# First key weights in three transfers, first x block in four parts, and a newly found order of work

## The chip, the cores and the metric

The kernel runs on one core of one Trainium2 chip. The metric is the device time of one execution in microseconds (us). It is given as the median of several runs. A profile is one execution recorded by the hardware profiler. It has a span, from the first to the last instruction, and an own time a little longer than the span.

A core has five engines with an instruction queue each: TensorE (PE in the views, with PEld for its weight loads), VectorE (DVE), ScalarE (ACT), GpSimd (POOL) and SyncE (SP). ACT and SP also issue DMA transfers here.

## The reference

The input x has 2048 tokens of 512 features in bf16. The output mixes two branches of the same x by a gate for each token:

```python
g = _sigmoid((x * gate_w).sum(-1, keepdims=True))
a = _A_ref(x, A_wq, A_wk, A_wv, A_wo, A_beta)
b = _B_ref(x, B_w_gate, B_w_up, B_w_down)
return g * a + (1 - g) * b
```

Branch A is attention with 32 heads of 16 features in four segments of 512 tokens. In each segment there is causal softmax attention inside the segment, and a read of a memory that the earlier segments have filled:

```python
logits = jnp.einsum('bhqd,bhkd->bhqk', qs, ks) * scale + mask
a_dot = jnp.einsum('bhqk,bhkd->bhqd', _softmax(logits, axis=-1), vs)
a_mem = (phi(qs) @ M) / (phi(qs) @ z + 1e-06)     # M, z: sums over earlier segments
o = g * a_mem + (1.0 - g) * a_dot                 # g = sigmoid(beta), for each head
M, z = M + phi(ks)^T @ vs, z + sum(phi(ks))
```

Here phi(t) is t + 1 where t is positive and exp(t) elsewhere. The heads are joined and multiplied by wo. Branch B is a gated feed-forward layer of width 1792: (gelu(x @ w_gate) * (x @ w_up)) @ w_down.

## The kernel before

The kernel is a list of some thousand small tasks. Each task is one step on one engine and is a handful of instructions. The functions below create the tasks. A long string, ORDER, gives the sequence in which they are written to the queues: each engine's queue holds its own tasks in the sequence of that string, and waits on semaphores are worked out from what each instruction reads and writes. A word such as `K0_1a:1` opens a PSUM bank (bank 1 of four, psD0 to psD3), and `Kev0_1:d` says that this eviction runs on DVE (`:a` is ACT).

The names of tasks carry the segment first. For segment s there are:

- `ld_...`: loads. x of segment 0 comes in two ways. Its tokens 0 to 255 come as rows (`ld_x0_0` on SP, `ld_x0_1` on ACT) and are transposed by PE (`xtr0_`) and copied out (`xev0_`, line 795). Its tokens 256 to 511 come through two DMA transposes (`ld_x0_t2`, `ld_x0_t3`, line 361). The other segments come through DMA transposes (`ld_x1_2` and so on, line 345). Line 341 issues every plain load.
- `warm1` and `warm2` (line 383): matmuls on constants, for no result.
- `K`, `Q`, `V`, `G`, `U`: projections, four matmuls of 512 columns each (V: two halves of 256 columns). In segment 0 the key tile K0_t is cut into a (blocks 2 and 3 of the input features, first 256 tokens), b (blocks 0 and 1, first 256 tokens) and c (all blocks, last 256 tokens); these are the matmuls of line 477. `Kev`, `Qev`, `Vev`, `Gev` evict the PSUM bank (lines 442 and 443, 506 and 507).
- `kpada`, `kpadb` (line 488): keys with alternate heads masked out, on DVE, one pair for each key tile.
- `st` (line 602) fills the four-bank score tile psX, `exp` (line 609) takes the exponential of all 2048 columns on ACT, `msk` (line 615) applies the causal mask on POOL. psX exists once, so st, exp, st, exp run in turn, 18 times for each segment.
- `pv` (line 644): probabilities times values for two key tiles; `tp`, `pvp`, `ota`, `otm` normalise and turn the result on DVE.
- `phka`, `phkb`, `phkc` and `phq...`: phi of keys and queries (DVE, ACT, DVE). `ktr`, `otr`: DMA transposes on SP. `mz`, `mza`, `mzq`: the update of the memory. `nd`, `ndp`: the read of it. `vsh`: a shifted copy of the values by DMA.
- `gelu`, `gd` on ACT; `h` (line 720) on DVE; `out` (line 735) is the down projection, `wo` (line 749) the output projection, `wev`, `oev` combine both, `dma` stores 128 tokens.
- `gwz` (line 354, DVE) clears a small tile, into which `ld_gw` loads the gate weights; `gwtr` on PE turns them.

In the string before, SP's loads begin x0_0, wk1, x0_t2, x0_t3, wq0, wq1, gw, wv, wg0, then x of segment 1; ACT's begin x0_1, wk0, wg0b. `wk1` holds blocks 2 and 3 of the key weights, `wk0` blocks 0 and 1.

Of the kernel before, what the change touches and what calls it, by code (L numbers as in the profile page):

```python
# [248 lines left out]
def _build(es, nc, A_x, A_wq, A_wk, A_wv, A_wo, A_beta, B_w_gate, B_w_up, B_w_down, gate_w, out):  # L249
# [90 lines left out]
    def ld_w(name, eng, dst, src, writes, size, wait=(), **kw):  # L340
        load(name, eng, lambda e: e.dma_start(dst, src), writes, size=size, wait=[("ld", w) for w in wait], **kw)
# [40 lines left out]
    for name, n, cols in (("warm1", 45, 80), ("warm2", 7, 80)):  # L382
        one(name, PE, 3.0, [I(lambda e, cols=cols: e.matmul(BK[s0.i][:, 0:cols], ones, ones[:, 0:cols], start=True, stop=True),  # L383
                              [], [bk(s0)]) for _ in range(n)], bias=9000.0, opens=name == "warm1")
# [400 lines left out]
    for p in (1, 0):  # L785
        one(f"xtr0_{p}", PE, 4 * T_TR, [I(lambda e, q=q, kb=kb, p=p: e.transpose(
            XB[:, 1024 * p + (kb % 2) * 256 + q * 128:1024 * p + (kb % 2) * 256 + q * 128 + 128],
            pt[stage[0]][:, q, kb * 128:(kb + 1) * 128], ident[:, :]),
            [("xs", 0, 0), ("xs", 0, 1), ("pt", stage[0]), ("ident",)], [("X", p)]) for kb in (2 * p, 2 * p + 1) for q in (0, 1)])
# [3 lines left out]
        task(f"xev0_{p}", [  # L793
            (ACT, 0.477, [I(lambda e, dst=dst, xin=xin: e.activation(dst, xin, ACTF.Copy), [("X", p)], wr)]),
            (DVE, 0.335, [I(lambda e, dst=dst, xin=xin: e.tensor_copy(dst, xin), [("X", p)], wr)])], L_DVE)
# [149 lines left out]
```

## Time and profile before

| | |
|---|---|
| median of 3 runs | 263.94 us (263.4 to 263.95) |
| profiled execution, own time | 264.41 us |
| its span | 262.7 us |
| busy: PE, DVE, ACT, POOL | 254.5, 198.1, 203.2, 98.3 us |
| HBM read, written | 7.87 MB, 2.10 MB |
| exp on ACT (L609) | 72 of 1.88 us, 135.1 us in all |
| masks on POOL (L615) | 128 of 0.73 us, 91.7 us in all |

A row of a timeline gives the start, the time taken, the engine, the line of the kernel, the operation, what it writes and reads, and a count; in brackets stands the idle time before it and what ended that. An engine with a q behind its name is the queue that issues DMAs. A row of a group gives busy time and the mean duration in ns behind the bar, then idle time before such instructions. The duration of a matmul includes its way through the array, so that matmuls in a row overlap: their spacing is read from their starts. In a table of stretches each column after the length is busy time with a count in brackets, then the granted TensorE clock, the DMA share and GB/s. A landing time counts from the issue of a transfer to the end of its last piece.

### The profile page before, as it was taken

To read this page: it belongs to the slowest core of one execution; us is meant where nothing else is said; L and a number is where in the kernel's file an instruction comes from. 1 tells how busy PE (TensorE), PEld (TensorE's weight loads), DVE (VectorE), ACT (ScalarE), POOL (GpSimd) and SP (SyncE) were. 2 spreads that over 40 slices of the span, in tenths; PEclk is the share of its full clock that TensorE was granted. 3 is DMA by queue.
4 is the path that set the end of the run, shared out by engine and by line. 5 is a ranking of instruction groups with operands and counts; after the bars stand their busy time and mean duration, and the time that the engine had idled before them with its cause. 6 is when DMAs were issued, how large, how long until landed. Compare 5 with 4: busy or idle time off the path is not lost.

```text
span 262.7 us, 6672 instructions
## 1 busy us (share of the span) xinstructions
PE 254.5 (97%) x2815; PEld 122.6 (47%) x2849; DVE 198.1 (75%) x412; ACT 203.2 (77%) x171; POOL 98.3 (37%) x163
## 2 busy tenths in 40 slices
...
DMA packets 31990, 16.50 MB, mean 63 GB/s; under 512 B 21592, under 2 KB 31960, under 8 KB 31960
## 3 DMA queue, kind: packets, MB, share of 16 engines
...
q10 hardware_dynamic: 688, 0.85, 0.9%
q8 instruction: 22, 0.36, 0.6%
...
HBM read 7.87 MB, written 2.10 MB: 38 GB/s over the span
## 4 chain that ended last, share of the span: by engine, by line
PE 88%; DVE 6%; ACT 3%; issue 2%; DVEq 0%
PE psD L449 41%; PE psD L735 19%; PE psX L602 8%; PE psD L644 6%; PE psD L749 5%; PE psD L499 5%; PE psD L547 1%; ACT gb L698 1%; PE psD L383 1%; PE psD L477 1%; DVE kT L443 1%; DVE gb L443 1%; ACT pt L609 1%; PE psD L577 1%; DVE phk L461 1%
## 5 line engine op out<-in xcount | busy, mean ns | idle before, releaser
L609 ACT ACTIVATE pt<-psX 128x2048 bf16<-128x2048 f32 x72 | 135.1, 1877 | 28.3 <-PE psX L602 26.7
L615 POOL TENSOR_TENSOR pt<-pt,ctri 128x256 bf16<-128x256 bf16 x128 | 91.7, 727 | 129.4 <-ACT pt L609 124.9
L449 PE MATMUL psD<-xT,wu 128*128 128x512 bf16 x214 | 52.7, 380 | 1.3 <-issue 1.1
L449 PE MATMUL psD<-xT,wg 128*128 128x512 bf16 x216 | 52.3, 379 | 0.8 <-issue 0.3
L735 PE MATMUL psD<-wd,gb 128*128 128x512 bf16 x217 | 51.8, 379 | 0.8 <-issue 0.5
L720 DVE TENSOR_TENSOR gb<-psD,gb 128x512 bf16<-128x512 f32 x56 | 37.2, 681 | 10.8 <-PE psD L449 10.8
L449 PEld LDWEIGHTS psD<-xT,wg 128*128 128x128 bf16 x224 | 20.7, 98 | 24.7 <-issue 1.3
L735 PEld LDWEIGHTS psD<-wd,gb 128*128 128x128 bf16 x224 | 20.7, 98 | 24.3 <-issue 2.1
L449 PEld LDWEIGHTS psD<-xT,wu 128*128 128x128 bf16 x224 | 20.2, 98 | 24.8 <-issue 2.6
L602 PE MATMUL psX<-qT,kD 32*128 32x192 bf16 (+7 forms) x512 | 28.5, 287 | 0.0
L530 DVE STREAM_TRANSPOSE tT<-psD 128x512 f32<-128x512 f32 x32 | 21.7, 701 | 5.5 <-PE psD L644 5.0
L443 DVE CAST gb<-psD 128x512 bf16<-128x512 f32 x20 | 13.6, 687 | 12.8 <-PE psD L449 12.8
L602 PEld LDWEIGHTS psX<-qT,kD 32*128 32x128 bf16 x512 | 8.2, 92 | 25.1 <-ACT pt L609 13.6
L499 PE MATMUL psD<-wv,xT 128*128 128x257 bf16 (+1 forms) x128 | 18.2, 273 | 0.0
L753 DVE SCALAR_TENSOR_TENSOR ost<-psD,gtok,wds 128x512 bf16<-128x512 f32 (+1 forms) x17 | 11.9, 710 | 7.9 <-PE psD L749 7.8
L668 DVE SCALAR_TENSOR_TENSOR ob<-tT,gq,rc 128x256 bf16<-128x256 f32 x32 | 16.7, 522 | 1.1
L703 ACT ACTIVATE gb<-psD 128x512 bf16<-128x512 f32 x28 | 15.0, 595 | 3.3 <-PE psD L449 3.3
L644 PE MATMUL psD<-pt,vsh 64*17 64x192 bf16 (+7 forms) x512 | 17.1, 283 | 0.0
L644 PE MATMUL psD<-pt,vnat 64*17 64x192 bf16 (+7 forms) x512 | 17.1, 283 | 0.0
L449 PE MATMUL psD<-xT,wq 128*128 128x512 bf16 x60 | 15.6, 379 | 0.4 <-issue 0.2
L749 PE MATMUL psD<-wo,oT 128*128 128x512 bf16 (+1 forms) x66 | 15.7, 367 | 0.2 <-issue 0.2
L499 PEld LDWEIGHTS psD<-wv,xT 128*128 128x128 bf16 x128 | 11.8, 97 | 6.6 <-issue 1.3
...
## 6 DMA issues: line engine op xcount, KB each, us to landing
out_dram<-ost SPq DMA_DIRECT2D x15, 128.0 KB, 1.9
...
wq<-in_A_wq_dram SPq DMA_DIRECT2D x2, 256.0 KB, 3.7
wv<-in_A_wv_dram SPq DMA_DIRECT2D x1, 512.0 KB, 3.8
wo<-in_A_wo_dram SPq DMA_DIRECT2D x1, 512.0 KB, 4.2
```

The source lines that it names most:

```text
L443: (DVE, 0.60, [I(lambda e: e.tensor_copy(dst, src()), [bk(sl), *reads], writes)]),
L449: one(name, PE, n * T_MM, [I(lambda e, i=i: e.matmul(BK[sl.i][:, :], lhs(i), rhs(i), start=(i == 0), stop=(i == n - 1)), reads(i), [bk(sl) ...
L499: one(f"V{s}_{m}{'ab'[hf]}", PE, 2 * T_MM, [I(lambda e, i=i, sl=sl, a=a, z=z, xs=xs: e.matmul(BK[sl.i][:, 0:z - a], xs(i), wv[:, i, a:z], ...
L530: one(f"tp{name}", DVE, 0.605, [I(lambda e, sl=sl, ti=ti: e.transpose(tT[ti][:, :], BK[sl.i][:, :]), [bk(sl)], [("tT", ti)])], bias=bias)
L602: ins.append(I(lambda e, t=t, kb=kb, ncol=ncol, c0=c0, g=g: e.matmul(XALL[:, g * 512 + c0:g * 512 + c0 + ncol], kD[(4 * s + t) % R_KD][32 ...
L609: one(f"exp{s}_{name}", ACT, 2048 * 0.000833 + 0.05, [I(lambda e: e.activation(pt[slot][:, :, :], xin, ACTF.Exp, scale=ATT_SCALE), [("X",) ...
L615: ins.append(I(lambda e, mv=mv: e.tensor_tensor(mv, mv, cm, ALU.mult), [("pt", slot), ("causal",)], [("pt", slot)]))
L644: ins.append(I(lambda e, kb=kb, slot=slot, c0=c0, n=n, g=g, r0=r0, sl=banks[j], va=va: e.matmul(BK[sl.i][32 * g:32 * g + 17, 64 * kb:512], ...
L668: I(lambda e, ti=ti, ri=ri, t=t, j=j, dst=dst: e.scalar_tensor_tensor(out=dst, in0=t_rows(ti), scalar=gq[:, 2 * t + j:2 * t + j + 1], in1= ...
L720: one(f"h{s}_{ft}", DVE, 0.605, [I(lambda e, sl=sl, gi=gi, f=f: e.tensor_tensor(gb[gi][:, f, :], BK[sl.i][:, :], gb[gi][:, f, :], ALU.mult ...
L735: mm.append(I(lambda e, fb=fb, gi=gi, f=f, q=q, sl=sl: e.matmul(BK[sl.i][:, :], gb[gi][:, f, q], wd[:, fb, :], start=(fb == 0), stop=(fb = ...
L749: one(f"wo{s}_{qt}{sfx}", PE, 4 * T_MM * w / 512, [I(lambda e, kb=kb, q=q, so=so, c=c, w=w: e.matmul(BK[so.i][:, 0:w], oT[:, kb, q], wo[:, ...
```

## The change

The key weights of blocks 2 and 3 are no longer one transfer on SP: block 2 stays there (`wk2`, 128 KB), block 3 goes to ACT (`wk3`, 128 KB), and blocks 0 and 1 (`wk0`, 256 KB) follow as ACT's third transfer. The two halves of the first x, `xtr0_1` and `xtr0_0` with one copy of 512 columns each, become four parts with one copy of 256 columns each, in four banks of psX; two of these copies run on ACT. The warm-up is one group of 52 matmuls of 66 columns in place of 45 and 7 of 80. ORDER is replaced as a whole. In the new string 46 evictions and copies run on ACT and 66 on DVE, where it was 35 and 75. Of the transfers, `gw` now follows `wg0`, `ktr0_0` comes early on SP, `ld_wo` comes after `vsh2_01`, and several `ktr`, `otr` and `vsh` trade places.

```diff
--- before.py
+++ after.py
@@ -355,8 +355,8 @@
     xin0 = A_x[0, 0:512, :].rearrange("(q p) d -> p q d", p=P)
     for eng, nm, q in ((SP, "0", slice(0, 1)), (ACT, "1", slice(1, 2))):
         ld_w(f"x0_{nm}", eng, pt[stage[0]][:, q, :], xin0[:, q, :], [("xs", 0, q.start)], 0.125)
-    for eng, h in ((SP, 1), (ACT, 0)):
-        ld_w(f"wk{h}", eng, wk[:, halves[h], :], wsrc(A_wk)[:, halves[h], :], [("wk", 2 * h), ("wk", 2 * h + 1)], 0.25)
+    for eng, nm, c in ((SP, "2", slice(2, 3)), (ACT, "3", slice(3, 4)), (ACT, "0", slice(0, 2))):
+        ld_w(f"wk{nm}", eng, wk[:, c, :], wsrc(A_wk)[:, c, :], [("wk", i) for i in range(c.start, c.stop)], 0.125)
     for q in (2, 3):
         load(f"x0_t{q}", SP, lambda e, q=q: e.dma_start_transpose(xT[0][:, :, 128 * q:128 * q + 128], A_x[0, 128 * q:128 * q + 128, :]),
              [("xT", 0, f"t{q}")], issue=1.31, lat=3.0)
@@ -379,9 +379,8 @@
 
     s0 = Slot()
     ones = nc.const_aps.tensor(1.0, [P, P], BF)
-    for name, n, cols in (("warm1", 45, 80), ("warm2", 7, 80)):
-        one(name, PE, 3.0, [I(lambda e, cols=cols: e.matmul(BK[s0.i][:, 0:cols], ones, ones[:, 0:cols], start=True, stop=True),
-                              [], [bk(s0)]) for _ in range(n)], bias=9000.0, opens=name == "warm1")
+    one("warm1", PE, 3.0, [I(lambda e: e.matmul(BK[s0.i][:, 0:66], ones, ones[:, 0:66], start=True, stop=True),
+                             [], [bk(s0)]) for _ in range(52)], bias=9000.0, opens=True)
     cn = [
         I(lambda e: e.memset(maskA[:], 0.0), writes=[("maskA",)]),
     ]
@@ -782,17 +781,15 @@
             I(lambda e: e.tensor_scalar(gfull[:], gfull[:], 1.0, None, ALU.add), [("gfull",)], [("gfull",)])], bias=-150.0)
 
     XB = XALL.bitcast(BF)
-    for p in (1, 0):
-        one(f"xtr0_{p}", PE, 4 * T_TR, [I(lambda e, q=q, kb=kb, p=p: e.transpose(
-            XB[:, 1024 * p + (kb % 2) * 256 + q * 128:1024 * p + (kb % 2) * 256 + q * 128 + 128],
+    for kb in (2, 3, 0, 1):
+        one(f"xtr0_{kb}", PE, 2 * T_TR, [I(lambda e, q=q, kb=kb: e.transpose(
+            XB[:, 1024 * kb + q * 128:1024 * kb + q * 128 + 128],
             pt[stage[0]][:, q, kb * 128:(kb + 1) * 128], ident[:, :]),
-            [("xs", 0, 0), ("xs", 0, 1), ("pt", stage[0]), ("ident",)], [("X", p)]) for kb in (2 * p, 2 * p + 1) for q in (0, 1)])
-        dst = xT[0][:, 2 * p:2 * p + 2, 0:256]
-        xin = XB[:, 1024 * p:1024 * p + 512].rearrange("p (k c) -> p k c", c=256)
-        wr = [("xT", 0, kb, "h0") for kb in (2 * p, 2 * p + 1)]
-        task(f"xev0_{p}", [
-            (ACT, 0.477, [I(lambda e, dst=dst, xin=xin: e.activation(dst, xin, ACTF.Copy), [("X", p)], wr)]),
-            (DVE, 0.335, [I(lambda e, dst=dst, xin=xin: e.tensor_copy(dst, xin), [("X", p)], wr)])], L_DVE)
+            [("xs", 0, 0), ("xs", 0, 1), ("pt", stage[0]), ("ident",)], [("X", kb)]) for q in (0, 1)])
+        dst, xin, wr = xT[0][:, kb, 0:256], XB[:, 1024 * kb:1024 * kb + 256], [("xT", 0, kb, "h0")]
+        task(f"xev0_{kb}", [
+            (ACT, 0.38, [I(lambda e, dst=dst, xin=xin: e.activation(dst, xin, ACTF.Copy), [("X", kb)], wr)]),
+            (DVE, 0.25, [I(lambda e, dst=dst, xin=xin: e.tensor_copy(dst, xin), [("X", kb)], wr)])], L_DVE)
 
     head_gates()
     for s in range(NSEG):
 ORDER = """
-ld_x0_0 ld_wk1 ld_x0_1 warm1:0 ident xtr0_1 xev0_1:d xtr0_0 warm2 xev0_0:d vones0 masks ld_wk0 causal1 gwz ld_x0_t2 ld_x0_t3 ld_wq0 ld_wq1 ld_gw
-causal0 consts K0_1a:1 K0_3a:2 K0_3b K0_2a:3 K0_0a:0 K0_2b K0_0b K0_1b K0_0c K0_2c K0_3c K0_1c Kev0_0:d Kev0_2:d kpadb0_0 kpadb0_2 causal kpada0_0
-Kev0_3:a Q0_0:0 ld_wg0b Qev0_0:a Q0_1:3 st0_0A gwtr:2 Kev0_1:d gwev Q0_3:0 ld_wv ld_wg0 Qev0_1:d V0_1b:1 V0_3a:2 V0_3b:3 exp0_0A Qev0_3:d Vev0_3a:a
-Vev0_1b:a st0_0B Vev0_3b:d kpada0_2 kpada0_1 V0_0b:0 V0_1a:2 V0_2a:1 Vev0_0b:d G0_6:3 Gev0_6:d Vev0_1a:d Vev0_2a:d exp0_0B st0_0C exp0_0C Q0_2:0
-G0_2:3 V0_2b:2 ld_x1_2 ld_x1_1 ld_x1_3 ld_x1_0 ld_beta st0_0D Vev0_2b:a exp0_0D Gev0_2:d kpadb0_1 Qev0_2:d phka0_0 V1_2b:1 V0_0a:3 G1_6:2 V1_0b:0
-Vev1_2b:d phka0_2 st0_0E Vev0_0a:d Vev1_0b:d G0_1:1 Gev1_6:a exp0_0E Gev0_1:d Q1_2:3 V1_3b:2 V1_3a:0 kpada0_3 Qev1_2:d Vev1_3a:d phkb0_2 phkc0_2
-Vev1_3b:d st0_1A gz0 exp0_1A gr0 Q1_0:1 V1_0a:3 G1_5:0 Vev1_0a:d Gev1_5:d st0_1B Q1_1:2 K1_0:3 exp0_1B phkb0_0 ld_wu1 ld_x2_0 G0_5:0 Qev1_0:d kpadb0_3
-vsh0_21 st0_1C exp0_1C Qev1_1:d ld_x2_1 ld_x2_3 ktr0_3 ld_wg1 Gev0_5:d V1_2a:1 K1_3:2 K1_1:0 vsh0_01 Vev1_2a:a vsh0_20 ld_x2_2 ktr0_2 vsh0_00 ld_wd1
-st0_1D phkc0_0 betab Kev1_1:d kpada1_1 G0_4:1 G0_3:0 Gev0_4:d Kev1_0:d Gev0_3:d Kev1_3:a ld_wd0 ld_wu0 ktr0_1 ktr0_0 vsh1_20 ld_wo V1_1a:2 Vev1_1a:d
-exp0_1D bexp st0_2A exp0_2A msk0_0B msk0_0D msk0_0C kpada1_0 msk0_0E goa0 gob0 msk0_0A msk0_1A msk0_1C msk0_1D gqa gfull msk0_1B G0_0:1 Q1_3:3 G1_1:0
-Qev1_3:d phqa1_0 st0_2B Gev0_0:d gqb Gev1_1:a pv0_1:2301 exp0_2B tp0_d01 tp0_d00 pvp0_01 Q2_0:3 Qev2_0:d tp0_d11 st0_2C K1_2:2 Kev1_2:d pvp0_00
-tp0_d10 gelu0 G0_8:3 G0_13:1 gd0_13 G0_10:2 G0_11:0 G0_9:1 gd0_8 gd0_10 gd0_9 gd0_11 G0_12:3 G0_7:2 gd0_12 G1_2:1 U0_0:0 gd0_7 Gev1_2:d pvp0_11 h0_0
-U0_13:3 U0_10:2 h0_10 Q2_1:1 Qev2_1:d exp0_2C st0_2D mz0:0 U0_7:2 U0_9:1 pvp0_10 h0_13 exp0_2D phqb1_0 st0_2E exp0_2E phka1_0 h0_7 mza0 h0_9 ota0_0
-phqa1_2 kpadb1_0 G1_4:3 U0_1:2 h0_1 Gev1_4:a V1_1b:0 st0_3A G1_0:1 U0_5:3 Q2_2:2 exp0_3A Vev1_1b:a Gev1_0:a Qev2_2:a kpadb1_1 st0_3B exp0_3B U0_11:0
...
+ld_x0_1 ld_wk3 ld_wk0 warm1:0 ld_x0_0 causal1 ident xtr0_2 xtr0_3 xtr0_0 xtr0_1 vones0 ld_wk2 ld_x0_t2 ld_x0_t3 ld_wq0
+xev0_3:d masks xev0_1:a xev0_0:a xev0_2:d K0_1a:1 K0_3a:2 K0_0a:3 K0_3b K0_1b K0_2a:0 K0_1c Kev0_1:d K0_3c Kev0_3:a
+kpadb0_1 kpadb0_3 K0_0b K0_0c K0_2b Kev0_0:a phka0_0 kpada0_0 gwz ld_wq1 ld_wg0b ld_wv ld_wg0 Q0_0:1 ld_gw Q0_2:2
+ld_x1_2 ld_x1_1 ld_x1_3 ld_x1_0 ld_beta ld_wu1 ld_x2_0 kpadb0_0 Qev0_0:a st0_0A exp0_0A K0_2c Q0_1:3 Qev0_1:d Q0_3:1
+st0_0B gwtr:3 Kev0_2:a gwev kpada0_2 V0_2a:0 Vev0_2a:d V0_1a:3 Vev0_1a:d Qev0_3:a V0_2b:1 V0_1b:0 Vev0_2b:d V0_0a:3
+Vev0_0a:d V0_0b:1 Vev0_0b:d Vev0_1b:d exp0_0B st0_0C V0_3b:3 Vev0_3b:d V0_3a:1 phkb0_0 Vev0_3a:d phkc0_0 ktr0_0
+vsh0_21 ld_x2_1 ld_x2_3 vsh0_01 ld_wg1 ld_x2_2 G0_6:0 G0_2:3 exp0_0C st0_0D exp0_0D Gev0_2:d Qev0_2:d G0_5:1 V1_2b:3
+G1_6:2 betab kpada0_1 Gev1_6:d st0_0E consts Vev1_2b:a G0_1:3 Q1_2:2 Gev0_6:a V1_3a:0 exp0_0E st0_1A causal0 causal
+msk0_0B msk0_0C Gev0_5:d msk0_0E Vev1_3a:d V1_0b:1 Q1_0:0 Qev1_2:a exp0_1A bexp gqa gfull G1_5:2 st0_1B Gev1_5:a
+Qev1_0:d Vev1_0b:d phka0_2 Gev0_1:d K1_0:0 Q1_1:1 V1_3b:2 V1_0a:3 exp0_1B msk0_1B Kev1_0:d kpada1_0 phkb0_2 st0_1C
+Qev1_1:d K1_1:0 V1_2a:1 Vev1_3b:d exp0_1C K1_3:2 Vev1_2a:a phkc0_2 st0_1D Kev1_1:d kpada1_1 G0_3:0 G0_4:1 vsh1_20
+vsh0_20 vsh0_00 ld_wd1 ktr0_2 exp0_1D Gev0_4:a kpadb0_2 st0_2A exp0_2A Vev1_0a:d kpada0_3 Gev0_3:d msk0_0D msk0_0A
+Q1_3:3 V1_1a:0 Vev1_1a:a G0_0:1 st0_2B Gev0_0:a msk0_1D Qev1_3:d phqa1_2 Kev1_3:d msk0_1A msk0_1C pv0_1:3021 gqb
+tp0_d01 Q2_0:0 tp0_d00 pvp0_01 exp0_2B K1_2:3 st0_2C Qev2_0:d tp0_d11 Kev1_2:d gelu0 pvp0_00 tp0_d10 ota0_0 pvp0_11
+pvp0_10 G0_11:0 gd0_11 G0_13:1 G0_9:3 gd0_9 G0_12:2 gd0_12 G0_8:0 gd0_8 gd0_13 G0_10:3 gd0_10 G0_7:2 gd0_7 msk0_2A
+G1_1:0 ktr0_3 ld_wd0 ld_wu0 ktr0_1 Q2_1:1 Qev2_1:d phka1_2 Gev1_1:d U0_0:3 U0_10:2 h0_10 U0_13:1 h0_0 h0_13 exp0_2C
+st0_2D exp0_2D U0_7:0 U0_9:2 mz0:3 st0_2E phka1_0 h0_7 h0_9 V1_1b:1 U0_1:0 h0_1 kpada1_2 G1_4:2 Gev1_4:d phkb1_0
+exp0_2E st0_3A Vev1_1b:a G1_0:0 Q2_2:1 U0_5:2 phqa1_0 exp0_3A gz1 msk0_2C gz0 phqb1_0 Qev2_2:a gr0 msk0_2E mza0 mzq0
+h0_5 Gev1_0:d st0_3B U0_12:3 G1_3:1 h0_12 Gev1_3:d U0_3:2 exp0_3B st0_3C msk0_2B gr1 goa1 h0_3 msk0_3B exp0_3C phkc1_0
+gob1 goc1 U0_4:0 U0_6:3 U0_11:1 h0_4 h0_6 h0_11 st0_3D U0_2:2 U0_8:0 kpadb1_0 phkb1_2 kpada1_3 h0_2 Q2_3:3 Qev2_3:d
+ktr1_1 vsh1_00 h0_8 G1_2:1 Gev1_2:d msk0_2D msk0_3A msk0_3C phqb1_2 exp0_3D st1_0A msk0_3D pv0_3:2301 exp1_0A st1_0B
...
-wev2_2:d h3_5 exp3_3B st3_3C exp3_3C wo2_2:2 out3_1_0:3 st3_3D out3_1_1 nd3_4:0 out3_1_2 dma8 exp3_3D msk3_3B msk3_2C msk3_3C msk3_3D wev3_1:a ota3_0
-ndp3_5 oev2_2 ndp3_4 ota3_1 dma11 otr3_2 otr3_1 otr3_3 otr3_0 pv3_3:1203 tp3_d20 tp3_d21 pvp3_20 pvp3_21 tp3_d30 tp3_d31 ota3_2 pvp3_31 pvp3_30 otm3_1
-otm3_0 ota3_3 out3_0_0:1 out3_2_0:2 out3_0_1 out3_2_1 out3_3_0:0 out3_0_2 out3_3_1 wev3_0:a otm3_2 otm3_3 wo3_0:3 dma10 oev3_0 dma12 wo3_1:1 out3_2_2
-out3_3_2 wo3_2:3 oev3_1 wev3_2:a oev3_2 wo3_3b:1 dma13 dma14 wev3_3:a oev3_3b dma15b wo3_3a:2 oev3_3a dma15a
...
+out2_2_2 nd3_3:1 ndp3_3 U3_5:3 nd3_5:0 h3_5 ndp3_5 exp3_3B st3_3C exp3_3C out3_1_0:1 wo2_2:3 pvp3_10 msk3_2E nd3_4:0
+st3_3D dma8 otr3_3 wev2_2:a ndp3_4 exp3_3D msk3_2D msk3_2B msk3_3B oev2_2 msk3_3C msk3_3A otr3_1 out3_1_1 out3_1_2
+wev3_1:a dma10 otr3_2 msk3_3D pv3_3:2031 ota3_0 ota3_1 tp3_d20 tp3_d21 dma11 otr3_0 pvp3_20 pvp3_21 tp3_d30 out3_3_0:2
+out3_0_0:0 out3_0_1 tp3_d31 ota3_2 pvp3_31 otm3_1 pvp3_30 otm3_0 ota3_3 otm3_2 out3_2_0:3 out3_2_1 out3_0_2 out3_3_1
+wev3_0:a otm3_3 wo3_0:1 oev3_0 wo3_1:0 out3_3_2 out3_2_2 wev3_2:a oev3_1 dma12 wo3_2:1 dma13 wo3_3b:0 oev3_2 dma14
+wo3_3a:3 wev3_3:a oev3_3b dma15b oev3_3a dma15a
 """
```

76 lines of the change are left out of this document (41 added, 35 removed).

## The prediction

> **What bounds the kernel now.** I read the page first: the busy row, then the chain of work that ended last.
>
> ```profile
> span 262.7 us, 6672 instructions
> PE 254.5 (97%) x2815; PEld 122.6 (47%) x2849; DVE 198.1 (75%) x412; ACT 203.2 (77%) x171; POOL 98.3 (37%) x163
> PE 88%; DVE 6%; ACT 3%; issue 2%; DVEq 0%
> ```
>
> TensorE (PE) is busy for 97% of the span and is 88% of the chain. An average hides where it is not busy, so the next view is PE's busy time by stretch, and then who made PE wait.
>
> ```profile
> 0.00:5.90 5.90, 4.48 (x60) 1.00 0.76 155
> 5.90:12.00 6.10, 6.04 (x45) 1.00 1.02 308
> 12.00:40.00 28.00, 27.68 (x245) 1.00 0.73 169
> 40.00:250.00 210.00, 206.65 (x2436) 1.00 0.19 39
> 250.00:262.70 12.70, 9.63 (x48) 1.00 0.21 61
> ...
> PE psD L449 <- issue: 1.8, 11, 0.2
> PE psD L477 <- DVE omem L354: 0.6, 1, 0.6
> ```
>
> From 5.90 to 250 PE lacks 3.7 us of 244.1 (6.10-6.04, 28-27.68, 210-206.65), in pieces of at most 0.2 us. So no order can win more than crumbs in the middle, and any order that makes PE wait there loses. What can be won lies ahead of 5.9 us (warm-up and transposes only) and behind 250 us. The change rebuilds the first, so the timeline of the head comes next.
>
> ```profile
> 0.79 0.40 SPq L341 DMA_DIRECT2D pt<-in_A_x_dram  x1
> 0.82 3.16 PE L383 MATMUL psD<-const-bfloat16-1.0 128*128 128x80 bf16 x45 [0.82 <-PEq L930]
> 1.22 0.46 ACTq L341 DMA_DIRECT2D wk<-in_A_wk_dram  x1
> 1.25 0.41 SPq L341 DMA_DIRECT2D wk<-in_A_wk_dram  x1
> 1.71 2.59 SPq L361 DMA_TRANSPOSE xT<-in_A_x_dram  x2
> 3.78 1.05 PE L786 MATMUL psX<-ident,pt 128*128 128x128 bf16 x8
> 4.44 0.85 DVE L795 COPY xT<-psX 128x512 bf16<-128x512 bf16 x2 [4.44 <-PE psX L786]
> 5.91 4.01 PE L477 MATMUL psD<-xT,wk 128*128 128x256 bf16 x32 [0.61 <-DVE omem L354]
> 9.97 1.67 PE L449 MATMUL psD<-xT,wq 128*128 128x512 bf16 x7
> 11.58 0.39 PE L602 MATMUL psX<-qT,kD 32*128 32x512 bf16 x4
> 12.03 1.88 ACT L609 ACTIVATE pt<-psX 128x2048 bf16<-128x2048 f32 x1 [0.61 <-PE psX L602]
> ...
> wk<-in_A_wk_dram ACTq DMA_DIRECT2D x1, 256.0 KB, 5.0
> wk<-in_A_wk_dram SPq DMA_DIRECT2D x1, 256.0 KB, 4.5
> pt<-in_A_x_dram ACTq DMA_DIRECT2D x1, 128.0 KB, 2.8
> DMA to landing us min/median/max: 4.2/4.6/5.0
> ```
>
> The last line is that of the two early DMA transposes into xT. x0_1 lands at 0.79+2.8 = 3.6 (its issue beside SP's at 0.79), wk1 at 1.25+4.5 = 5.75, wk0 at 1.22+5.0 = 6.22. The transposes were issued at 1.71 and about 3.0 and should land in turn, so I read 1.71+5.0 = 6.7 (x0_t2) and 3.0+4.2 = 7.2 (x0_t3). The copies of x end at 5.29, yet the first key matmul starts at 5.91, 0.16 after wk1 lands: the row blames the memset of omem, which ended at 5.9 by chance, but the last to come for the data is wk1.
>
> **The change, part by part.** *Head.* wk1 (256 KB) becomes wk2 on SP and wk3 on ACT, 128 KB each, at the same places in their queues; wk0 becomes third on ACT. The x copies go from two of 0.42 us on DVE to four, two on DVE and two on ACT. K0's first-half pieces (blocks 2 and 3) can then start once wk2, wk3 and two DVE copies are there. A 128 KB piece at the same place is bounded by x0's 2.8 us below (1.22+2.8 = 4.0) and by 4.5 us above (5.75); I take 5.1 for the start, set by the copies (transposes from 3.78, the first four by about 4.2, PE-to-DVE latency 0.2 as in the row at 4.44, two half copies of 0.25 to 0.42). So about 0.8 us earlier. But the new order puts only three first-half pieces (6 of the 32 matmuls) ahead of K0_3b, which needs wk0. What K0 gains is therefore set by wk0 and, two pieces later, by x0_t3, which K0_1c needs. The same bytes stand ahead of these landings as before (window row 5.90:12.00: DMA share 1.02, so bytes, not issues, set them). I keep 6.22 and 7.2; the bounds for wk0 are 5.75 (it takes the share wk1 had) and 7.2 (it shares with both transposes to their end).
>
> The rows show 32 key matmuls starting from 5.9 to 9.6, 0.12 each, and eight query matmuls from 9.97 to 11.58 less the latency, 0.21 each. New PE order: six matmuls, K0_3b K0_1b K0_2a (6), K0_1c K0_3c K0_0b K0_0c K0_2b (16), Q0_0 Q0_2 (8), then the first score fill st0_0A. By wk0: 6.22+0.14+22x0.12+8x0.21 = 10.7. By x0_t3: 7.2+0.14+16x0.12+8x0.21 = 10.9. By the key masks on DVE, which the new order puts behind the key feature step phka0_0:
>
> ```profile
> L442 ACT ACTIVATE kT<-psD 128x512 bf16<-128x512 f32 x5 | 3.0, 597 | 7.5 <-PE psD L477 6.5 <-PE psD L449 0.8 <-DVE phk L465 0.2
> L461 DVE TENSOR_SCALAR phk<-kT 128x1024 bf16<-128x1024 bf16 x6 | 2.9, 480 | 0.0
> L488 DVE TENSOR_SCALAR kD<-kT,maskB 128x512 bf16<-128x512 bf16 x16 | 5.6, 363 | 0.0
> L354 DVE MEMSET omem<- x1: 112/112/112, 5.8 to 5.8; 128x64 uint32 x1
> ```
>
> K0_0c ends at 7.34+14x0.12+0.2 = 9.2, then 0.60 (eviction on ACT) + 0.48 (phka0_0) + 0.36 + 0.11 (gwz) + 0.36 = 11.1. The latest wins: st0_0A at 11.1 instead of 11.58, -0.5 us. But K0_2c (4x0.12) is still owed then: +0.5. **Head: 0.0 net**, with ends from -0.5 (all landings early, DVE path 0.5 shorter) to +0.8 (wk0 at 7.2: 7.34+22x0.12+8x0.21 = 11.7, +0.1, +0.5 owed, and 0.2 for the pads behind it).
>
> *SyncE's queue.* gw moves behind wg0 and waits for gwz, now near 10.8; the four x1 transposes stand behind gw. They start near 11 instead of 10.63 and have some 9 us until V1_2b, which the new order puts even one gate tile later: nothing. ld_wo moves from 47 us to behind vsh2_01, some 85 us. Its cover is out0_0 (14 matmuls of 0.216), three K2 tiles (12) and two fills of 0.43, together 6.5 us after V2_0b; it needs two evictions, two issues of 0.4 to 0.6 and its landing:
>
> ```profile
> wo<-in_A_wo_dram SPq DMA_DIRECT2D x1, 512.0 KB, 4.2
> 31.16 1.88 ACT L609 ACTIVATE pt<-psX 128x2048 bf16<-128x2048 f32 x1 [0.20 <-PE psX L602]
> 32.93 0.38 ACT L507 ACTIVATE vnat<-psD 128x256 bf16<-128x256 f32 x1
> 33.20 0.60 ACT L442 ACTIVATE kT<-psD 128x512 bf16<-128x512 f32 x1
> 33.76 1.88 ACT L609 ACTIVATE pt<-psX 128x2048 bf16<-128x2048 f32 x1
> ```
>
> 1.2+1.1+4.2 = 6.5: no slack, 0 to 0.5 us if it slips; I count 0. The other moves on this queue, of the transposes ktr and otr and of the last x3 piece, keep several us of cover by the same count: nothing.
>
> *Middle.* Counting words of the two orders: the same fills in the same sequence, the same eight pv groups behind the same neighbours. Of the single-tile evictions, about nine more (some 5 us) stand on ACT and as much less on DVE. The rows above tell what ACT can hide: from one exp to the next ACT start 1.77, two small evictions (0.27+0.56), the next exp 2.60 after the first. So an exp-to-exp step of 2.60 hides 0.83 of small work; a fill step with 2.17 us of other PE work takes 2.60 as well. In the first segment the new order loads steps with 1.12, 0.98, 1.00, 0.81, 0.98 and 0.83; the excess over 0.83 is 0.29, 0.15, 0.17 and 0.15, and the following step mostly has PE work to spare. One place has too little: between st0_1D and st0_2A stand two dense tiles (1.73) where exp needs about 1.95: +0.2. Later double loads (phkb1_2 with phqb1_2, four evictions ahead of exp3_0B) are followed by longer steps. **Middle: +0.2**, from 0 to +1.0.
>
> *Tail.* After the last pv the row below holds in both orders: 34 down-projection matmuls cover the DVE chain to the output projection.
>
> ```profile
> 247.21 7.29 PE L735 MATMUL psD<-wd,gb 128*128 128x512 bf16 x33 [0.16 <-issue]
> 254.33 1.89 PE L749 MATMUL psD<-wo,oT 128*128 128x512 bf16 x8
> 256.06 1.89 PE L735 MATMUL psD<-wd,gb 128*128 128x512 bf16 x8
> 258.00 1.68 PE L749 MATMUL psD<-wo,oT 128*128 128x512 bf16 x11
> ```
>
> The new order swaps the last two down-projection blocks, and ota3_0, ota3_1 precede the transposes as before: 0, within 0.2 either way.
>
> **Sum:** 0.0+0.2+0.0 = +0.2 us. The profiled run took 264.41 us by its own time, 1.7 around its span, and lies 0.5 above the median of 263.94 (263.4 to 263.95). On the median: 264.1. A change of 0.2% (0.53 us) is about what a measurement of this kernel can tell from none.
>
> **The rivals.** *Faster.* The small pieces really land early: wk0 at 5.75, x0_t3 at 6.7. Then st0_0A is at 5.75+0.14+2.64+1.68 = 10.2 by PE and 10.6 by the masks; with 0.5 owed, and the mask stall filled, that is -0.5 to -0.9, 263.2. For it: each first part is half as long. Against: the DMA engines are full.
>
> *Slower, the exp chain.* If the steps of the first segment find no spare PE work, the excesses add up, 0.29+0.15+0.17+0.15 = 0.76, with the 0.2 at st0_2A: +1.0, 264.9. It decides once two loaded steps follow each other. For: the largest PE wait is 0.6 now because each step just fits; a new order fitted to estimates has more ways to miss. Against: DVE is relieved by as much.
>
> *Slower, the slow clock.* The head's matmuls run at half rate at first:
>
> ```profile
> L786 PE MATMUL psX<-ident,pt x8: 307/311/311, 3.8 to 4.5; 128*128 128x128 bf16 x8
> L477 PE MATMUL psD<-xT,wk x32: 272/273/421, 5.9 to 9.6; 128*128 128x256 bf16 x32
> ```
>
> The longest key matmul took 421 ns and the median 273: the fast rate came only within K0, after 5.9 us, with PE busy from 0.82 but for 0.6. The change drops warm2 and narrows warm1, and PE may idle from 4.6 to 5.1 and again before wk0. If that leaves the clock slow for the 26 other key matmuls, each costs 0.1 more (8 transposes of half the columns span 0.74 between starts, 0.106 each): +2.6 at the most, 1.3 if half of them, 265.4 on top of the forecast. [...]
>
> *It does not do what it says.* wk0, third on ACT, lands only with x0_t3 at 7.2: +0.8 in the head and the 0.2 of the middle, 264.9. [...]
>
> **How the numbers follow.** Forecast (within 0.2%) 0.42; early landing 0.26; exp chain 0.18; slow clock 0.08; late wk0 0.06. Hence faster 0.26, same 0.42, slower 0.32. The forecast alone spans 263.5 to 264.5. The range runs from 262.9 (early landing, -0.9, and 0.1 of scatter) to 265.6 (all slower cases, but the worst of the clock).
>
> **What would show it.** Right: first key matmul near 5.1, a pause before the seventh, st0_0A near 11.1, PE's share from 12 to 250 unchanged, 31 to 40 us with a wait of 0.2 before a fill. Wrong: st0_0A before 10.6 or after 11.8; key matmuls of 421 ns beyond the eighth; PE waits on ACT adding over 0.5 us; a PE wait at L749 near 93 us for wo.

## The result, and the profile after

The changed kernel takes 266.95 us (median of 6 runs, 265.23 to 268.47) against 263.39 us for the kernel before (6 runs, 263.02 to 263.95): ratio 1.0129, 95% interval 1.0079 to 1.0178. It is slower by 3.4 us by the ratio (3.6 between the medians). A ratio here compares mean times, without executions more than 1.5% above the fastest of the same kernel. The runs of the changed kernel spread over 3.2 us where those of the kernel before spread over 0.9. The profiled execution took 266.26 us by its own time, with a span of 264.5. Line numbers after the change are one lower (K 476, projections 448, scores 601, P·V 643, gwtr 768).

From the page of the changed kernel: span, busy row, shares of the chain, and the row of the instruction queue (packets, MB, share).

```profile
span 264.5 us, 6703 instructions
PE 258.2 (98%) x2849; PEld 122.0 (46%) x2849; DVE 195.6 (74%) x403; ACT 207.4 (78%) x182; POOL 97.0 (37%) x163
PE 95%; DMA 2%; ACT 1%; DVE 1%; issue 1%; DVEq 0%
...
q8 instruction: 22, 0.36, 0.6%
```

PE's busy sum cannot be set against the 254.5 of before, whose record lacks 34 matmuls. New is the 2% of DMA in the chain. The waits of PE say which (engine, line, waited for: us in total, times, longest):

```profile
PE psD L768 <- DMA omem<-in_gate_w_dram: 1.1, 1, 1.1
PE psD L643 <- issue: 0.9, 1, 0.9
PE psD L382 <- PEq L942: 0.8, 1, 0.8
PE psX L601 <- ACT pt L608: 0.2, 1, 0.2
PE psD L476 <- DVE xT L792: 0.2, 1, 0.2
```

The two largest rows are new against the kernel before. The first lies in the head, here from the timeline of the changed kernel:

```profile
4.85 3.65 PE L476 MATMUL psD<-xT,wk 128*128 128x256 bf16 x28 [0.16 <-DVE xT L792]
8.34 1.89 PE L448 MATMUL psD<-xT,wq 128*128 128x512 bf16 x8
9.74 0.33 SPq L341 DMA_DIRECT2D omem<-in_gate_w_dram  x1
10.16 0.39 PE L601 MATMUL psX<-qT,kD 32*128 32x512 bf16 x4
10.61 1.88 ACT L608 ACTIVATE pt<-psX 128x2048 bf16<-128x2048 f32 x1 [0.61 <-PE psX L601]
12.76 0.40 PE L601 MATMUL psX<-qT,kD 32*128 32x448 bf16 x8
14.25 0.18 PE L768 MATMUL psD<-ident,omem 128*128 128x4 bf16 x1 [1.10 <-DMA omem<-in_gate_w_dram]
14.35 2.79 PE L498 MATMUL psD<-wv,xT 128*128 128x256 bf16 x24
```

The gate weights, 1 KB, are issued at 9.74 behind wg0 and release PE at 14.25, 4.5 us later. `gwtr` (L768) is the first thing on PE behind the second fill, and the V matmuls stand behind it in the queue. The second new row is inside the P·V group pv3_1, again on the timeline:

```profile
224.23 0.40 PE L601 MATMUL psX<-qT,kD 32*128 32x448 bf16 x8
224.55 0.39 PE L643 MATMUL psD<-pt,vnat 64*17 64x512 bf16 x4
...
226.40 0.31 PE L643 MATMUL psD<-pt,vnat 64*17 64x320 bf16 x4
227.64 0.26 PE L643 MATMUL psD<-pt,vsh 64*17 64x192 bf16 x4 [0.93 <-issue]
...
227.95 1.04 PE L448 MATMUL psD<-xT,wu 128*128 128x512 bf16 x4
```

PE starts nothing from 226.41 to 227.64, in the second half of the group, and no semaphore is named ("issue"). The group takes 3.20 us from its first to its last start, where the other seven take 1.88 to 1.91.

To set the two kernels side by side, another execution of the kernel before was profiled (`before_again`, below). Against it, the start of the same exponential in the changed kernel is 0.60 us earlier at the first, 1.06 later at the third, 1.29 later at the start of the second segment, 1.40 later ahead of pv3_1 and 2.72 later behind it; the spans differ by 2.7 (264.5 to 261.8). So nearly the whole loss of this execution is in two places, and at both PE stands still.

### The profile page after: what moved, and what is told of

It reads as the page before. It is cut to its first block, busy times and chain, and to the rows that moved or that the text cites. A ratio compares the mean times of both kernels' runs of the same rounds, so it can differ in the third digit from the quotient of the medians.

```text
span 264.5 us, 6703 instructions
## 1 busy us (share of the span) xinstructions
PE 258.2 (98%) x2849; PEld 122.0 (46%) x2849; DVE 195.6 (74%) x403; ACT 207.4 (78%) x182; POOL 97.0 (37%) x163
## 4 chain that ended last, share of the span: by engine, by line
PE 95%; DMA 2%; ACT 1%; DVE 1%; issue 1%; DVEq 0%
PE psD L448 45%; PE psD L734 19%; PE psX L601 9%; PE psD L643 6%; PE psD L498 6%; PE psD L748 5%; DMA omem<-in_gate_w_dram 2%; PE psD L476 1%; PE psD L546 1%; PE psD L382 1%; ACT pt L608 1%; PE psD L576 1%; DVE ost L752 0%; ACT kT L441 0%; DVE xT L792 0%
## 5 line engine op out<-in xcount | busy, mean ns | idle before, releaser
L614 POOL TENSOR_TENSOR pt<-pt,ctri 128x256 bf16<-128x256 bf16 x128 | 89.1, 707 | 128.4 <-ACT pt L608 105.2
L448 PE MATMUL psD<-xT,wu 128*128 128x512 bf16 x224 | 54.7, 380 | 0.0
L719 DVE TENSOR_TENSOR gb<-psD,gb 128x512 bf16<-128x512 f32 x56 | 37.9, 685 | 21.5 <-PE psD L448 21.1
L734 PE MATMUL psD<-wd,gb 128*128 128x512 bf16 x224 | 53.5, 380 | 0.0
L448 PE MATMUL psD<-xT,wg 128*128 128x512 bf16 x224 | 53.0, 379 | 0.0
L702 ACT ACTIVATE gb<-psD 128x512 bf16<-128x512 f32 x28 | 15.6, 594 | 3.1 <-PE psD L448 2.8
L498 PE MATMUL psD<-wv,xT 128*128 128x256 bf16 (+1 forms) x128 | 17.9, 273 | 0.0
L739 ACT ACTIVATE wds<-psD,omgt 128x512 f32<-128x512 f32 x7 | 4.7, 685 | 12.6 <-PE psD L734 12.6
```

What stands on the lines that cost most here:

```text
L448: one(name, PE, n * T_MM, [I(lambda e, i=i: e.matmul(BK[sl.i][:, :], lhs(i), rhs(i), start=(i == 0), stop=(i == n - 1)), reads(i), [bk(sl) ...
L498: one(f"V{s}_{m}{'ab'[hf]}", PE, 2 * T_MM, [I(lambda e, i=i, sl=sl, a=a, z=z, xs=xs: e.matmul(BK[sl.i][:, 0:z - a], xs(i), wv[:, i, a:z], ...
L614: ins.append(I(lambda e, mv=mv: e.tensor_tensor(mv, mv, cm, ALU.mult), [("pt", slot), ("causal",)], [("pt", slot)]))
L702: t = one(f"gd{s}_{ft}", ACT, 0.485, [I(lambda e, gi=gi, f=f, sl=sl: e.activation(gb[gi][:, f, :], BK[sl.i][:, :], ACTF.Gelu_apprx_tanh), ...
L719: one(f"h{s}_{ft}", DVE, 0.605, [I(lambda e, sl=sl, gi=gi, f=f: e.tensor_tensor(gb[gi][:, f, :], BK[sl.i][:, :], gb[gi][:, f, :], ALU.mult ...
L734: mm.append(I(lambda e, fb=fb, gi=gi, f=f, q=q, sl=sl: e.matmul(BK[sl.i][:, :], gb[gi][:, f, q], wd[:, fb, :], start=(fb == 0), stop=(fb = ...
```

## The experiments

Theory A: PE stands still because small loads that it or a copy ahead of it needs come late in the new sequence. Theory B: PE stands still because its own instructions come late into a dense group. Rivals: the new head, the exp chain, masks.

**The same kernel again, and the new head alone.** `after_again` is the changed kernel without an edit. `head_only` has the three key pieces, four x parts and one warm-up in the ORDER of before:

```diff
-ld_x0_0 ld_wk1 ld_x0_1 warm1:0 ident xtr0_1 xev0_1:d xtr0_0 warm2 xev0_0:d vones0 masks ld_wk0 causal1 gwz
+ld_x0_0 ld_wk2 ld_x0_1 ld_wk3 ld_wk0 warm1:0 ident xtr0_2 xtr0_3 xtr0_0 xtr0_1 xev0_3:d xev0_1:a xev0_0:a xev0_2:d vones0 masks causal1 gwz
```

> The changed kernel as it is, profiled again. Theory A (gate weights late): the PE wait at the gate turn (L768) is there in every execution, near 1.1 us, since the load stands behind the two first gate-projection loads. Theory B (a hole in PE's instruction supply inside pv3_1, 1.2 us without a semaphore wait): the hole at 226.4 us comes back at the same place, and its length, or further holes, explain why the runs differ by 3 us. Rival C: the hole is a chance event of one execution and is gone here; then the spread of the runs has another cause.

> The order of before with only the new head: key weights in three transfers, x in four parts, one warm-up group. Its gate-weight load stays early. If the head is good by itself, K0 starts near 4.9 and the first score fill comes 0.5 to 1.2 us earlier than 11.58, and the time is 0.5 to 1.0 us below before (262.4 to 262.9); theory B expects no hole, so a spread below 1 us. Rival: the old order of K0 pieces needs wk0 after four matmuls and the earlier start is lost: within 0.3 us of before.

`after_again`: 267.64 us (265.4 to 270.56), ratio 1.0124 [1.0093, 1.0154]. Its profiled execution is the slowest of the six (270.56), so it shows how far the wait can go and not what it costs as a rule. A row of the waits of PE:

```profile
PE psD L768 <- DMA omem<-in_gate_w_dram: 3.7, 1, 3.7
```

And three stretches of the same execution (length, busy PE, PEld, DVE, ACT, POOL, then granted clock, DMA share, GB/s):

```profile
12.00:17.00 5.00, 1.29 (x14) 0.35 (x12) 0.69 (x1) 4.29 (x5) 0.00 (x0) 0.88 1.42 125
17.00:20.30 3.30, 3.30 (x17) 2.33 (x18) 1.73 (x6) 0.00 (x0) 0.00 (x0) 0.50 0.61 121
20.30:26.00 5.70, 5.70 (x43) 2.97 (x42) 3.73 (x11) 1.93 (x2) 0.00 (x0) 0.79 0.45 156
```

The same wait is 3.7 us instead of 1.1, from 13.27 to 16.98. The granted clock falls to 0.50 inside it: if it has only the values 0.50 and 1.00, which is assumed, the means of 0.88 and 0.79 put the slow stretch at 15.8 to 22.7 (an estimate). In the stretch at 0.50, 17 matmuls take 3.30 us, 0.19 each, where the row at 14.35 above has 24 V matmuls in 2.79 us, 0.12 each. In this execution pv3_1 has no hole (2.08 us), against theory B's expectation. The length of the gate wait and the hole both differ between the two executions, so both add to the spread; two profiles cannot show that they are all of it.

`head_only`: 263.77 us (263.47 to 264.06), ratio 1.0 [0.9991, 1.0009]. In the old order the new loads and copies cost nothing and bring nothing, as the rival had it: PE starts the key matmuls early and then waits for wk0 (first row of its waits).

```profile
PE psD L476 <- DMA wk<-in_A_wk_dram: 0.8, 1, 0.8
```

**The gate weights early, with 52 and with 92 warm-up matmuls.** `gw_early` puts gwz and ld_gw of the changed ORDER back to about where the kernel before had them; `gw_early_92` also cuts the same warm-up columns into more matmuls, so that only the number of instructions on PE differs.

```diff
-... xtr0_1 vones0 ld_wk2 ld_x0_t2 ld_x0_t3 ld_wq0 xev0_3:d ... kpada0_0 gwz ld_wq1 ld_wg0b ld_wv ld_wg0 Q0_0:1 ld_gw Q0_2:2
+... xtr0_1 vones0 gwz ld_wk2 ld_x0_t2 ld_x0_t3 ld_wq0 ld_wq1 ld_gw xev0_3:d ... kpada0_0 ld_wg0b ld_wv ld_wg0 Q0_0:1 Q0_2:2
 (gw_early_92 only)
-ones[:, 0:66] ... range(52)
+ones[:, 0:36] ... range(92)
```

> The changed kernel with the clearing of omem right after vones0 and the gate-weight load back behind wq1, where it stood before the change; nothing else. Theory A: the wait of 1.1 us at L768 goes, exp 0_0C to 1_0A come 1.1 to 1.3 us earlier, the median falls by 1.1 us or a little more, from 267.0 to about 265.8. Rival: the wait is hidden work, another wait (value evictions, exp) takes its place, and less than 0.4 us is gained.

> As gw_early, but the warm-up is 92 matmuls of 36 columns in place of 52 of 66: 40 more matmuls and 40 more weight loads stand ahead of everything else in PE's instruction stream, so the blocks in which instructions are fetched end 40 pairs earlier in the program; the work is the same. Theory B: the hole in pv3_1 goes or moves to another place, and the time falls by up to 1.2 us below gw_early. Rival C: no difference to gw_early beyond what a longer or shorter warm-up gives at the head (read from the first score fill).

`gw_early`: 266.21 us (264.87 to 267.39), ratio 1.0089 [1.0062, 1.0115]. That is 0.7 us under the changed kernel where theory A expected 1.1, and it is not clear of the scatter. The gate wait is gone, but another takes its place (timeline, DVE and PE):

```profile
21.95 0.74 DVE L763 COPY betab<-omem 32x8 bf16<-32x8 bf16 x4 [1.39 <-DMA omem<-in_A_beta_dram]
22.72 0.35 DVE L487 TENSOR_SCALAR kD<-kT,maskA 128x512 bf16<-128x512 bf16 x1
...
23.13 0.29 PE L601 MATMUL psX<-qT,kD 32*128 32x256 bf16 x4 [1.08 <-DVE kD L487]
```

`betab` waits on DVE for beta, another small load (8 KB, issued at 16.97); the masked keys kpada0_1 stand behind it, and the fifth fill waits for them. The hole in pv3_1 is there as well (3.53 us).

`gw_early_92`: 271.98 us (270.01 to 273.63), ratio 1.0305 [1.0271, 1.034]: 5.8 us more for 40 more pairs of matmul and weight load that fit into the same warm-up time, where a fall of up to 1.2 us was expected. pv3_1 has no hole (2.09 us), and three other places have holes instead (timeline):

```profile
43.23 0.27 PE L643 MATMUL psD<-pt,vnat 64*17 64x256 bf16 x1 [3.09 <-issue]
...
77.54 0.27 PE L643 MATMUL psD<-pt,vsh 64*17 64x256 bf16 x1 [0.62 <-issue]
...
169.51 0.37 PE L601 MATMUL psX<-qT,kD 32*128 32x448 bf16 x5 [1.12 <-issue]
```

**Beta's copy later, and three positions in PE's stream.**

```diff
-V1_2b:3 G1_6:2 betab kpada0_1 Gev1_6:d ... msk0_0E Vev1_3a:d V1_0b:1
+V1_2b:3 G1_6:2 kpada0_1 Gev1_6:d ... msk0_0E Vev1_3a:d betab V1_0b:1
 (gw_beta has 52 warm-up matmuls of 66 columns)
+gw_beta_44: ones[:, 0:78] ... range(44)
+gw_beta_60: ones[:, 0:57] ... range(60)
```

> gw_early with one more move: betab, VectorE's copy of the beta values, goes behind the eviction Vev1_3a, so that the padded keys kpada0_1 no longer stand behind a copy that waits for beta. Theory A (the waits for late small loads are what the change costs in the first 25 us): the 1.1 us of PE's wait at the fifth fill goes, the exponentials stand about 0.3 to 0.6 us ahead of the kernel before from the fifth on, and the time is 1.0 to 1.4 us under that of gw_early (266.2), so 264.8 to 265.2. Theory B (PE's own instructions come late at pv3_1) keeps a hole of 0.9 to 1.6 us there, which is why it is still above 263.65. Rival: the waits were covered by work that is still owed, and the time stays at 266.2.

> gw_beta with the warm-up in 44 matmuls of 78 columns in place of 52 of 66: the same PE time before the first key matmul, 8 matmuls and 8 weight loads fewer in PE's stream. Theory B: what decides the hole is where in PE's stream of instructions a P*V group falls between two of the 16 KB fetches; with 16 instructions fewer the fetch that pv3_1 needs comes later against it, so the hole in pv3_1 changes in length by some tenths of a us or goes to another group, and the time moves by 0.5 to 2 us either way. Rival (the hole comes from masks, vsh or another wait, whatever the position in the stream): hole and time as in gw_beta within 0.3 us.

> gw_beta with the warm-up in 60 matmuls of 57 columns in place of 52 of 66: 8 matmuls and 8 weight loads more in PE's stream. Theory B: the hole in pv3_1 gets shorter or longer by some tenths of a us, or another group gets one, and the time moves by 0.5 to 2 us against gw_beta, on the other side of it from the version with 44. Rival (position in the stream is nothing): as gw_beta within 0.3 us.

`gw_beta`: 264.92 us (264.16 to 266.22), ratio 1.0051 [1.0031, 1.0071], 1.3 under `gw_early`, as theory A expected. At the start of the second segment its exponentials are 0.66 us behind `before_again`, where those of `gw_early` are 2.06 behind. Its profiled run still has the hole:

```profile
PE psD L643 <- issue: 1.2, 1, 1.2
...
PE psD L643 <- DMA vsh<-vnat: 0.3, 1, 0.3
```

`gw_beta_44`: 265.35 us, 1.0067 [1.0041, 1.0093], with a shorter hole (pv3_1 2.67 us). `gw_beta_60`: 264.26 us (263.86 to 265.63), 1.0033 [1.0016, 1.005], with none in the profiled run (2.08 us). The holes changed, but neither time is clear of the scatter of `gw_beta` (the intervals overlap), and 44 has the shorter hole with the longer time. So these two times do not decide between theory B and its rival.

**The kernel before with 40 more pairs.** If B holds, the order that has no holes must get them too.

```diff
-(("warm1", 45, 80), ("warm2", 7, 80))
+(("warm1", 85, 42), ("warm2", 7, 80))
```

> The kernel before with its second warm-up in 85 matmuls of 42 columns in place of 45 of 80, the same columns in all within 1%: 40 matmuls and 40 weight loads more in PE's stream, and nothing else. Theory B: PE gets holes of 1 to 3.5 us in one or more P*V groups that the kernel before does not have, without any wait for a semaphore, and the time is 1 to 6 us above it with a wider spread. Rival (holes belong to the new order of work): within 0.3 us of the kernel before.

268.72 us (267.94 to 270.63), ratio 1.0208 [1.0174, 1.0241]. The timeline has three holes that the kernel before has not, one in a P·V group and two in the fills right behind one:

```profile
42.86 0.28 PE L644 MATMUL psD<-pt,vnat 64*17 64x256 bf16 x4 [1.74 <-issue]
...
76.83 0.40 PE L602 MATMUL psX<-qT,kD 32*128 32x448 bf16 x7 [0.85 <-issue]
...
168.60 0.21 PE L602 MATMUL psX<-qT,kD 32*128 32x64 bf16 x3 [1.12 <-issue]
```

Against `before_again` the exponentials lose 1.9, 1.2 and 1.3 us at these three places, 4.4 in all. No order of work, load or semaphore differs, so the holes do not belong to the new order.

**What the holes follow.** The instruction queue moves 0.36 MB in 22 pieces of 16 KB, which is some 64 bytes for each of PE's 5,700 matmuls and weight loads; so I take it as PE's stream, and a piece as about 128 pairs of load and matmul (an estimate from these numbers). A P·V group is 128 pairs in 1.88 us. The packet records of the trace give when the piece that falls next to the start of pv3_1 is moved:

| kernel (profiled run) | piece starts, against the start of pv3_1 | pv3_1 takes, us |
|---|---|---|
| before, before_again, head_only, gw_late | 1.97, 2.39, 2.30, 2.41 ahead | 1.88 each |
| after_again, gw_beta_60 | 2.41 and 2.45 ahead | 2.08, 2.08 |
| gw_beta_44 | 0.04 ahead | 2.67 |
| after, gw_early, gw_beta | 0.38, 0.44, 0.45 behind | 3.20, 3.53, 3.46 |
| gb60_vsh, gb68_vsh | 0.42, 0.50 behind | 3.10, 3.69 |
| before_92, gw_early_92 | 9.5, 8.2 ahead, the next 1.9 behind | 1.88, 2.09 |

In the thirteen holes of 0.4 us and more, in the eight profiles that have any, PE goes on 1.2 to 1.7 us after the record of a 16 KB piece ends (after: piece from 224.93 for 1.35 us, PE again at 227.64; before_92: 40.35 for 1.09, again at 42.86). Stretches of the DMA view say the same: in the changed kernel no packet of q8 lies in 222.19:224.90, and in 224.90:227.64 stands

```profile
q8 instruction: 1, 0.02, 3.1%
```

PE's weight loads, counted in the traces, show where it stops. In all six profiles with a hole in pv3_1, with 44, 52, 60 or 68 warm-up matmuls, PE stops behind its 2508th weight load. The other seven holes stand behind load 472 to 474, 853 to 855 and 1871 to 1873. From one such place to the next are about 380, 1018 and 637 loads, near 3, 8 and 5 times 127. So the holes belong to fixed places in PE's stream, whole pieces apart, whatever work stands there. That is what one would expect, by my reading, if PE has used up one piece and the next is not there yet.

Such pieces are moved all through the run: by the packet records the first of the 22 starts at 12.16 us in the changed kernel and the last at 249.43.

**The gate weights' place alone, in the kernel before.**

```diff
-masks ld_wk0 causal1 gwz ld_x0_t2 ld_x0_t3 ld_wq0 ld_wq1 ld_gw causal0 ... kpada0_0 Kev0_3:a Q0_0:0 ld_wg0b Qev0_0:a ... Q0_3:0 ld_wv ld_wg0 Qev0_1:d
+masks ld_wk0 causal1 ld_x0_t2 ld_x0_t3 ld_wq0 ld_wq1 causal0 ... kpada0_0 gwz Kev0_3:a Q0_0:0 ld_wg0b ld_wv ld_wg0 ld_gw Qev0_0:a ... Q0_3:0 Qev0_1:d
```

> The kernel before with one thing of the change: gwz and ld_gw, the gate weights' clearing and load, stand behind kpada0_0 and behind ld_wg0 as they do in the changed kernel, so that the load is issued behind 0.9 MB of other weights. All else is as before. Theory A: the transpose gwtr, which this order has right behind the first score fill at 11.7 us, waits until the gate weights land at 14 to 17 us; PE stands for 2 to 5 us, no work that is owed fills it, and the time is 1.5 to 5 us above the kernel before with a wide spread. Rival (the gate weights land in time or the wait is covered): within 0.4 us of the kernel before.

266.07 us (265.71 to 268.59), ratio 1.0102 [1.0058, 1.0145]. The timeline:

```profile
10.60 0.39 PE L602 MATMUL psX<-qT,kD 32*128 32x512 bf16 x4
13.28 0.18 PE L769 MATMUL psD<-ident,omem 128*128 128x4 bf16 x1 [2.29 <-DMA omem<-in_gate_w_dram]
```

After this wait every exponential to the end is 2.19 us later than in `before_again`. So one moved load of 1 KB, with its clearing, costs 2.2 us in the old order; the changed kernel lost 3.4. In the three executions with the late load it comes about when the big ones ahead of it do: PE goes on 0.2 to 0.3 us after the half of wg that ACT issued (448 KB) has landed, which was at 13.05 here, at 14.09 in `after` and at 16.67 in `after_again`.

**Both remaining waits out, and another position.** `gb60_vsh` is `gw_beta_60` with two moves; `gb68_vsh` has 68 warm-up matmuls of 50 columns besides. `before_again` is the kernel before, unchanged.

```diff
-... ld_wg1 ld_x2_2 G0_6:0 ... G0_4:1 vsh1_20 vsh0_20 vsh0_00 ld_wd1 ... exp3_2A msk3_2A msk3_1D wev2_3:a
+... ld_wg1 ld_x2_2 vsh0_20 vsh0_00 G0_6:0 ... G0_4:1 vsh1_20 ld_wd1 ... exp3_2A msk3_1D msk3_2A wev2_3:a
```

> gw_beta_60 with two moves: vsh0_20 and vsh0_00, the shifted copies of V that pv0_1 reads, are issued on SyncE's queue right behind ld_x2_2 in place of behind vsh1_20, and the mask msk3_1D stands ahead of msk3_2A on GpSimd's queue. If what the new order still loses against the kernel before is these two waits (0.4 us for vsh in pv0_1, 0.2 us for the mask at pv3_1), the exponentials from the third slab on stand 0.4 to 0.6 us ahead of those of gw_beta_60 and the time is 263.6 to 263.9, level with the kernel before (263.55). If the hole in pv3_1 comes back (theory B leaves that open, as PE reaches the group earlier against the fetch), 264.5 to 265.5. Rival (the two waits are covered): 264.3.

> gb60_vsh with the warm-up in 68 matmuls of 50 columns in place of 60 of 57: 8 matmuls and 8 weight loads more in PE's stream, no other edit. In the profile of gb60_vsh the new order was within 0.15 us of the kernel before up to the fill ahead of pv3_1, and all it lost was the hole in that group. Theory B: the boundary between two fetched pieces falls earlier in the program by 8 pairs, so the fetch that pv3_1 needs starts ahead of the group more often; 263.6 to 264.2 with fewer runs above 265. If another group now has a hole instead, 264.5 to 266. Rival (the position is nothing, the hole belongs to the order): 265.5 as gb60_vsh.

> The kernel before, once more, unchanged: its first profile had the first key matmul at 5.9 us and a span of 262.7 us. If that head was 0.3 to 0.7 us later than usual (as the versions with an unchanged head or less suggest, whose exponentials all stand 0.26 to 0.6 us ahead of it from the first to the last), the span comes out at 262.0 to 262.4 and the first fill at 10.9 to 11.3 in place of 11.58. Otherwise 262.7 again.

`gb60_vsh`: 265.46 us (263.92 to 267.35), 1.0061 [1.0032, 1.009]; `gb68_vsh`: 265.74 us (264.89 to 267.73), 1.0081 [1.0059, 1.0102]. The vsh wait is gone, and most exponentials of `gb60_vsh` stand 0.16 to 0.19 us behind those of `before_again` from the second segment to pv3_1; but the hole is back in both (one row of `gb60_vsh`, two of `gb68_vsh`):

```profile
226.28 0.31 PE L643 MATMUL psD<-pt,vsh 64*17 64x320 bf16 x4 [1.04 <-issue]
```

```profile
44.64 1.67 PE L448 MATMUL psD<-xT,wg 128*128 128x512 bf16 x7 [1.53 <-issue]
...
228.91 0.23 PE L643 MATMUL psD<-pt,vnat 64*17 64x128 bf16 x4 [1.63 <-issue]
```

My reading that 8 pairs more steer a hole out of pv3_1 has fallen: `gw_beta_60` had a fetch in time, its two sisters had not. By the count above the place lies inside pv3_1 for every warm-up tried, so 8 pairs cannot move it out. What settles whether a piece starts 2.4 us ahead of the group or 0.4 us behind its start stays open; `after` and `after_again`, the same program, have one each.

`before_again`: 263.55 us, span 261.8. Its head:

```profile
5.10 4.00 PE L477 MATMUL psD<-xT,wk 128*128 128x256 bf16 x32
9.15 1.67 PE L449 MATMUL psD<-xT,wq 128*128 128x512 bf16 x7
10.76 0.40 PE L602 MATMUL psX<-qT,kD 32*128 32x512 bf16 x4
11.09 0.18 PE L769 MATMUL psD<-ident,omem 128*128 128x4 bf16 x1
```

All its exponentials are 0.82 to 0.85 us ahead of those in the first profile of before, from the first on: that execution had a late head and nothing else. Its first loads were late: the two halves of wk landed at 5.78 and 6.22, and at 4.69 and 5.13 in `before_again`. No version tried beats the kernel before.

## Why the prediction was wrong, point by point

*SyncE's queue: the step that failed.* It moved gw behind wg0, saw the wait for gwz, priced what is queued behind gw on SP, and wrote "nothing". It did not ask who reads gw. With its own figures gw lands at 10.8 plus 4.2 to 5.0, near 15.5, while gwtr stands on PE right behind the second fill, at 11.1+0.3+0.5+1.7+0.3 = 13.9: a wait of 1 to 2 us could have been worked out. It measured 1.1 and 3.7 us in two executions and 2.3 with the move alone (`gw_late`, 263.74 to 266.07). The forecast of 264.1 with 2.3 more is 266.4, above the range by itself. In `before_again`, with gw issued at 5.93, gwtr ran at 11.09 without a wait. The new place of betab on DVE, not priced either, was hidden behind gw's wait and showed as 1.1 us once that was gone. The same step's ld_wo at 0 held: PE does not wait at the output projection.

*PE's instructions: a term that was missing.* No view that I read named a cost for them, and the sum had no place for it. In the profiled run pv3_1 takes 1.32 us longer than in the kernel before (3.20 less 1.88). Of this 0.20 is a wait for a mask, which `after_again` has without a hole (2.08), and 1.12 the hole. With that the difference of the spans adds up, by the offsets against `before_again`: 0.60 early at the first exponential; 1.66 lost up to the third, which is the gate wait (1.1) and K0_2c then owed (4 matmuls, 0.5); 0.23 up to the second segment; 0.11 up to pv3_1; 0.20 and 1.12 in it; 0.03 won behind it: -0.60+1.66+0.23+0.11+0.20+1.12-0.03 = 2.69.

*Head, net 0.0: near in sum, wrong in its parts.* The first key matmul came at 4.85 and the first fill at 10.16, as in the rival "Faster" (10.2), not at 11.1; a fill before 10.6 was among the prediction's own signs of being wrong. The landings were mis-sized: wk0 landed at 5.58 and x0_t3 at 6.46, not at 6.22 and 7.2, which came from one execution with late loads. The start of 5.91 in that execution was late too: `before_again`, at 263.55 us near the median, has 5.10, and the fill at 10.76. Against that the gain was 0.6 and the debt 0.5, so two errors cancelled, and that the net came out near 0.0 is in part luck. `head_only`, with the new loads in the old order, measured 1.0 [0.9991, 1.0009].

*Middle, +0.2: right.* The 0.2 before st0_2A is in the waits of the changed kernel, and with the small waits removed `gb60_vsh` is 0.16 to 0.19 behind over most of the middle. The exp chain did not add up to 1 us. *Tail, 0 within 0.2: right* (-0.03). One reading was off without changing the sum: the 3.7 us that PE seemed to lack from 5.90 to 250 is mostly missing records. `head_only`, with the old order behind the head and all 2849 matmuls on record, has three waits of PE in its list, all in the head.

*The slow clock*, which the tables of stretches do not show in the head (granted 1.00 there in both kernels), cost K0 nothing more than before by the durations: two of its matmuls took over 300 ns (396 and 331), where it was four in the profile of before (421 twice, 373 and 361). It came elsewhere, inside and behind PE's wait of 3.7 us, at 0.50. The waits of 1.1 us (`after`) and 2.3 us (`gw_late`) left the clock at 1.00, in the wait and in the stretch behind it; in the wait of 3.7 us it fell after some 2.5 us, by the estimate of 15.8 above. What makes it fall was not shown.

*The range* (262.9 to 265.6) left out 266.95 because each slower rival was a single late step in work I had listed; none was a load read by PE or the supply of instructions.
